# A weights' conversion on VectorE: shift and bitwise or in one instruction, for a shift and an integer addition

## The chip, the cores and the metric

The kernel runs on one core of one Trainium2 chip. The metric is device time in microseconds (us) for one execution of the whole program; where several executions are given, their median counts.

## The reference

Two parts follow each other. The first is a recurrent attention (RWKV-6): batch 4, 8 heads, 768 steps, 48 columns a head. The second is a dense block over the resulting 3072 tokens of 384 columns, with 2048 hidden columns. The weights of the dense block, `w_in` and `w_out`, arrive as 64-bit floats.

```python
for t in range(S):                       # for each batch b and head h
    y[t]  = r[t] @ (state + outer(u * k[t], v[t]))
    state = w[t][:, None] * state + outer(k[t], v[t])
x = y.transpose(...).reshape(3072, 384)
h = x @ w_in                             # 384 -> 2048
out = (h - tanh(h)) @ w_out              # 2048 -> 384
```

## The kernel before, in words

**Blocks.** The work is cut into 8 blocks of 384 tokens (4 batches, two halves of the sequence each). A block's dense part is a loop over `f` from 0 to 15, each `f` being 128 hidden columns. One step `f` does the following:

- TensorE multiplies the block's input by the weights `w_in` of this `f` (`first`, tile `hp`, L718: six matmuls of 128x384).
- ScalarE moves the product out of PSUM (tile `h`, L721). Only one `hp` tile exists, so the next step's `hp` matmuls need this move done.
- VectorE takes the square and its maximum (tile `s`, L747); ScalarE squares again (tile `qa`, L750); VectorE forms two products (tiles `h` and `sums`, both L724). The result approximates `h - tanh(h)`.
- Two steps later (`LAG`) TensorE multiplies this by `w_out` (`Second.add`, tile `acc`, L795: six matmuls).

In blocks 2 to 7 most of that second product uses fewer, recombined matmuls (L833). The change doesn't touch that.

**Attention between the steps.** While block `i` runs its dense loop, the attention of block `i+1` is spread over the same sixteen steps. The function `plan` says at which `f` each piece is issued: on VectorE the scans (L374, L385), products (L392, L399), the update of the states (L506, L516) and masked copies (L452); on ScalarE scalings (L410), copies (L471) and bounds (L416); on TensorE small matmuls (L445, L469, L494, L559, L576). A first stage, `boot`, does this for block 0 ahead of everything.

**The weights.** They are converted from 64-bit floats to 32-bit floats on the chip, once, slice by slice: `load_weights` (L240) brings slice `f`, 128 partitions x 768 numbers of 64 bits, as tile `raw` (five buffers), and `convert` turns it into `w_sb[:, f]`. ScalarE does three passes over 768 columns (all L253): the high word scaled into `w_sb`, the sign into the upper half of each word of tile `up`, and the low word, scaled and rounded to a small integer, into the lower half of `up`. VectorE then shifts `w_sb` left by 3 bits (L257) and adds `up` as integers (L258). Slices 0 to 2 are converted in `boot`, slice 3 begins there, and slices 4 to 15 are converted during block 0: at step `f` (from 1 on) ScalarE issues its three passes for slice `f + 3`, and VectorE's part is issued one step later, behind that step's square (L747). So `w_sb[:, 11]`, say, is finished on VectorE shortly before the `hp` matmuls of step 11 read it.

**Order.** The order of instructions on TensorE, VectorE, ScalarE and the SyncE queue is the order in which the program issues them (`manual_schedule`). Each engine works in order, and semaphores join the engines. The loads of later slices are held until the move `h` of their step (`begin_behind`).

Of the kernel before, what the change touches and what calls it, by code (L numbers as in the profile page):

```python
# [39 lines left out]
U32 = mybir.dt.uint32  # L40
# [5 lines left out]
AF = mybir.ActivationFunctionType  # L46
ALU = mybir.AluOpType
# [39 lines left out]
UPSCALE = 2.0 ** 8  # L87
HIGH_SCALE = 2.0 ** -111
SIGN_SCALE = 2.0 ** -64
LEAST = 2.0 ** -24  # L90


# [27 lines left out]
def kernel(  # L120
# [12 lines left out]
    nc = tc.nc  # L133
# [109 lines left out]
    def convert(f, raw, _):  # L243


        lo, hi = raw[:, :, 0], raw[:, :, 1]
        a = w_sb[:, f, :].bitcast(I32)
        up = conv.tile([P, 2 * DM], I32, name="up", tag="up", bufs=4)
        low, high = (up.bitcast(t).rearrange("p (n two) -> p n two", two=2)[:, :, i]
                     for i, t in enumerate((U16, F16)))  # L250

        def scaled(to, of, scale):
            return lambda: nc.scalar.activation(out=to, in_=of, func=AF.Copy, scale=scale)  # L253

        return [scaled(a.bitcast(F32), hi.bitcast(F32), HIGH_SCALE), scaled(high, hi.bitcast(F32), SIGN_SCALE),
                scaled(low, lo.bitcast(U32), 2.0 ** -29)], [
                lambda: nc.vector.tensor_single_scalar(a, a, 3, op=ALU.logical_shift_left),  # L257
                lambda: nc.vector.tensor_tensor(out=a, in0=a, in1=up, op=ALU.add)]  # L258

    def scratch(ps):  # L260
        return ps.tile([P, 2, BANK], F32, name="att", tag="att")
# [17 lines left out]
    class Block:  # L279
# [123 lines left out]
        def take_whole(self, p0, n):  # L403
            t = self.half("post", p0, n * NCH * LP).rearrange("d (c j) -> d c j", j=LP)[:, :, 1]
            nc.vector.tensor_single_scalar(self.whole(p0, n), t, LEAST, op=ALU.max)

# [12 lines left out]
        def held(self, p0, n):  # L419
            i = (self.b * NQ + self.q) * NPAIR * NCH  # L420
            nc.vector.tensor_single_scalar(holds[:, i + p0 * NCH:i + (p0 + n) * NCH], self.whole(p0, n), LEAST,
                                           op=ALU.is_gt)
# [506 lines left out]
    def boot(ps, blk, later):  # L929
# [34 lines left out]
        blk.times_before(h2, UP)  # L964
        blk.update_1(ps)
        first_a, first_b = convert(*raws.pop(0))
        second_a, second_b = convert(*raws.pop(0))
        third_a, third_b = convert(*raws.pop(0))
        run(first_a)
        own()  # L970
# [158 lines left out]
    for op in ahead_of_h + rest:  # L1129
        op()  # L1130
    nc.vector.tensor_single_scalar(again, sure[0:1, 0, 0:1], float(P * (n_whole + n_excess + n_top)),
                                   op=ALU.not_equal)
# [71 lines left out]
```

## Time and profile before

| what | value |
|---|---|
| time, median of 3 runs | 578.82 us (576.56 to 578.95) |
| time of the profiled execution | 575.73 us |
| its span, first to last instruction | 574.0 us |
| TensorE (PE) busy | 554.2 us, 97% |
| VectorE (DVE) busy | 486.3 us, 85% |
| ScalarE (ACT) busy | 345.4 us, 60% |
| granted TensorE clock | 1.000 |
| VectorE's shift, L257 | 16 times, 8.9 us |
| VectorE's integer addition, L258 | 16 times, 15.3 us |
| ScalarE's three passes, L253 | 48 times, 46.3 us |

The busy times belong to the whole span. All conversions lie between 16 and 92 us of it. A time in the profile is the duration of an instruction from its start to its end; two instructions on one engine can overlap a little, so that the distance from one start to the next is shorter than the duration.

### The profile page before, as it was taken

To read this page: it belongs to the slowest core of one execution; us is meant where nothing else is said; L and a number is where in the kernel's file an instruction comes from. 1 tells how busy PE (TensorE), PEld (TensorE's weight loads), DVE (VectorE), ACT (ScalarE), POOL (GpSimd) and SP (SyncE) were. 2 spreads that over 40 slices of the span, in tenths; PEclk is the share of its full clock that TensorE was granted. 3 is DMA by queue.
4 is the path that set the end of the run, shared out by engine and by line. 5 is a ranking of instruction groups with operands and counts; after the bars stand their busy time and mean duration, and the time that the engine had idled before them with its cause. 6 is when DMAs were issued, how large, how long until landed. Compare 5 with 4: busy or idle time off the path is not lost.

```text
span 574.0 us, 14058 instructions
## 1 busy us (share of the span) xinstructions
PE 554.2 (97%) x5736; PEld 405.6 (71%) x5736; DVE 486.3 (85%) x942; ACT 345.4 (60%) x702; POOL 11.9 (2%) x40
## 2 busy tenths in 40 slices
PE   4899999999999999999999999999999999999996
PEld 4646656566665787777878787778878777777763
DVE  8899995799979988979899898989999998658673
ACT  3889884433236765577565774767556775667441
POOL 6100000000000000000000000000000000000000
PEclk9999999999999999999999999999999999999999
DMA  8595454221302232032222232122221300100101
GB/s 312 184 377 175 166 166 123 82 83 56 112 12 84 83 112 61 8 120 62 58 65 83 84 106 63 53 82 70 88 66 49 120 2 2 44 10 1 42 2 45
DMA packets 32453, 50.40 MB, mean 88 GB/s; under 512 B 2560, under 2 KB 30336, under 8 KB 32384
## 3 DMA queue, kind: packets, MB, share of 16 engines
q1 hardware_dynamic: 32144, 49.38, 26.8%
q8 instruction: 46, 0.75, 0.5%
q14 instruction: 23, 0.19, 0.1%
q0 software_dynamic: 96, 0.07, 0.1%
q10 hardware_dynamic: 144, 0.00, 0.0%
HBM read 43.55 MB, written 4.72 MB: 84 GB/s over the span
## 4 chain that ended last, share of the span: by engine, by line
PE 87%; DVE 7%; ACT 3%; issue 1%; DMA 1%; SPq 0%; DVEq 0%
PE hp L718 40%; PE acc L833 22%; PE acc L795 10%; PE att L833 5%; PE att L445 3%; PE att L559 2%; PE att L494 2%; PE att L469 2%; PE att L576 2%; DVE w_sb L258 1%; ACT up L253 1%; DMA r<-in_rT 1%; DVE sums L724 1%; DVE w_sb L257 1%; DVE s L747 1%
## 5 line engine op out<-in xcount | busy, mean ns | idle before, releaser
L718 PE MATMUL hp<-xT,w_sb 128*128 128x384 f32 x768 | 270.3, 488 | 3.2 <-ACT h L721 1.4
L718 PEld LDWEIGHTS hp<-xT,w_sb 128*128 128x128 f32 x768 | 138.3, 190 | 83.6 <-ACT h L721 6.3
L721 ACT ACTIVATE h<-hp 128x384 f32<-128x384 f32 x128 | 62.6, 489 | 150.6 <-PE hp L718 149.2
L833 PE MATMUL acc<-forms,g 128*128 128x128 f32 x810 | 121.1, 277 | 0.5
L833 PEld LDWEIGHTS acc<-forms,g 128*128 128x128 f32 x810 | 108.7, 192 | 15.6 <-issue 1.2
L765 DVE TENSOR_TENSOR g<-g 128x256 f32<-128x256 f32 x225 | 95.5, 424 | 19.8 <-PE acc L833 0.9
L724 DVE SCALAR_TENSOR_TENSOR h<-h,s 128x384 f32<-128x384 f32 x128 | 70.4, 550 | 10.2 <-ACT s L739 9.6
L795 PE MATMUL acc<-w_sb,sums 128*128 128x384 f32 x192 | 68.0, 490 | 0.9 <-DVE sums L724 0.7
L724 DVE SCALAR_TENSOR_TENSOR g<-qa,h 128x384 f32<-128x384 f32 x96 | 53.6, 558 | 17.5 <-PE acc L833 4.0
L740 ACT ACTIVATE qa<-s,shift 128x384 f32<-128x384 f32 x90 | 55.4, 615 | 3.0
L742 ACT ACTIVATE junk<-s,shift 128x384 bf16<-128x384 f32 x90 | 53.9, 599 | 0.0
L795 PEld LDWEIGHTS acc<-w_sb,sums 128*128 128x128 f32 x192 | 35.7, 190 | 24.9 <-DVE sums L724 1.5
L739 ACT ACTIVATE s<-h 128x384 f32<-128x384 f32 x90 | 47.1, 523 | 2.8
L833 PE MATMUL acc<-w_sb,g 128*128 128x128 f32 x270 | 44.8, 275 | 0.0
L750 ACT ACTIVATE qa<-s,shift 128x384 f32<-128x384 f32 x38 | 23.4, 615 | 25.5 <-DVE top L747 25.5
L833 PEld LDWEIGHTS acc<-w_sb,g 128*128 128x128 f32 x270 | 37.4, 192 | 0.0
L253 ACT ACTIVATE up<-raw 128x768 f16<-128x768 f32 (+1 forms) x32 | 31.8, 1061 | 0.0
L747 DVE CUSTOM_DVE_ANT_0 s<-h 128x384 f32<-128x384 f32 x38 | 21.0, 553 | 11.6 <-ACT h L721 11.6
L833 PE MATMUL att<-w_sb,g 128*128 128x128 f32 x180 | 30.2, 275 | 0.0
L833 PEld LDWEIGHTS att<-w_sb,g 128*128 128x128 f32 x180 | 26.4, 192 | 4.5
L374 DVE TENSOR_TENSOR_SCAN pre<-w,start 128x780 f32<-128x780 f32 x16 | 28.5, 1782 | 0.6
L385 DVE TENSOR_TENSOR_SCAN post<-w,seed 128x780 f32<-128x780 f32 x16 | 28.5, 1783 | 0.1
(88 smaller groups left out, 529.3 us busy)
## 6 DMA issues: line engine op xcount, KB each, us to landing
raw<-in_weights SPq DMA_DIRECT2D x16, 768.0 KB, 4.5
w<-in_wT SPq DMA_DIRECT2D x7, 780.0 KB, 4.5
k<-in_kT SPq DMA_DIRECT2D x7, 768.0 KB, 4.6
r<-in_rT SPq DMA_DIRECT2D x7, 768.0 KB, 4.5
v_sb<-in_v SPq DMA_DIRECT2D x8, 576.0 KB, 4.3
k<-in_tokens SPq DMA_DIRECT2D x6, 576.0 KB, 3.9
r<-in_tokens SPq DMA_DIRECT2D x6, 576.0 KB, 3.9
out_y<-sums SPq DMA_DIRECT2D x15, 128.0 KB, 1.9
```

Source lines behind the costliest of these rows:

```text
L253: return lambda: nc.scalar.activation(out=to, in_=of, func=AF.Copy, scale=scale)
L374: return nc.vector.tensor_tensor_scan(out=self.tile("pre")[:, cols], data0=self.tile("w")[:, cols], data1=start[:, 0:n * NCH * LP], initia ...
L385: return nc.vector.tensor_tensor_scan(out=back(t[:, 0:width]), data0=back(self.tile("w")[:, a:a + width]), data1=back(seed[:, 0:width]), i ...
L718: nc.tensor.matmul(hp, lhsT=w_in_sb[:, f, kc, :], rhs=xT[kc], start=(kc == KC - 1), stop=(kc == 0))
L721: return h, nc.scalar.activation(out=h, in_=hp, func=AF.Copy, scale=1.0 / UPSCALE)
L724: return lambda: nc.vector.scalar_tensor_tensor(out=out, in0=in0, scalar=scalar, in1=in1, op0=op0, op1=ALU.mult)
L739: nc.scalar.activation(out=s, in_=h, func=AF.Square)
L740: nc.scalar.activation(out=qa, in_=s, func=AF.Square, bias=shift[:, 4:5])
L742: nc.scalar.activation(out=junk[:, 0:NB], in_=s, func=AF.Relu, bias=shift[:, 5:6], accum_out=excess[:, at:at + 1])
L765: return lambda: nc.vector.tensor_tensor(out=G[:, to:to + 2], in0=two(G, g_at(q, a0), g_at(q, a1)), in1=two(G, g_at(q, b0), g_at(q, b1)), ...
L795: nc.tensor.matmul(acc, lhsT=g[:, j * P:(j + 1) * P], rhs=w_out_sb[:, f, :], start=(f == self.first), stop=(f == NF - 1))
L833: nc.tensor.matmul(to, lhsT=G[:, g_at(q, a), :], rhs=rhs, start=start, stop=stop, skip_group_check=True)
```

## The change

The two VectorE instructions of `convert` become one, `scalar_tensor_tensor`, which shifts `w_sb` left by 3 and combines the result with `up` by a bitwise or. An addition lets the low word carry into the upper bits when it rounds up to 8; an or does not. So the low word is brought to 0 to 7: ScalarE's pass over it multiplies by 0.90625 x 2^-29 in place of 2^-29 and adds 0.2499, a constant inside the same instruction.

```diff
+LOW = 0.90625 * 2.0 ** -29, 0.2499
...
-        def scaled(to, of, scale):
-            return lambda: nc.scalar.activation(out=to, in_=of, func=AF.Copy, scale=scale)
+        def scaled(to, of, scale, bias=0.0):
+            return lambda: nc.scalar.activation(out=to, in_=of, func=AF.Copy, scale=scale, bias=bias)
 
         return [scaled(a.bitcast(F32), hi.bitcast(F32), HIGH_SCALE), scaled(high, hi.bitcast(F32), SIGN_SCALE),
-                scaled(low, lo.bitcast(U32), 2.0 ** -29)], [
-                lambda: nc.vector.tensor_single_scalar(a, a, 3, op=ALU.logical_shift_left),
-                lambda: nc.vector.tensor_tensor(out=a, in0=a, in1=up, op=ALU.add)]
+                scaled(low, lo.bitcast(U32), *LOW)], [
+                lambda: nc.vector.scalar_tensor_tensor(out=a, in0=a, scalar=3, in1=up, op0=ALU.logical_shift_left,
+                                                       op1=ALU.bitwise_or)]
```

VectorE's stream loses 16 instructions; the order of all others, and the streams of TensorE, ScalarE, GpSimd and SyncE, stay the same. From `convert` on, line numbers grow by two: L718 is L720 in the changed kernel.

## The prediction

> **What bounds the kernel now.** I read the busy times and slices first: which engine is full, and where.
>
> ```profile
> PE 554.2 (97%) x5736; PEld 405.6 (71%) x5736; DVE 486.3 (85%) x942; ACT 345.4 (60%) x702; POOL 11.9 (2%) x40
> ...
> PE   4899999999999999999999999999999999999996
> ...
> DVE  8899995799979988979899898989999998658673
> ```
>
> TensorE is full almost everywhere. The change acts only where conversions run, 24 to 92 us, so I next read stretches of 12 us there (busy us of each engine in brackets' order PE, weight load, DVE, ACT, POOL).
>
> ```profile
> 36.00:48.00 12.00, 11.30 (x43) 6.80 (x42) 11.62 (x20) 10.64 (x16) 0.00 (x0) 1.00 0.86 312
> 48.00:60.00 12.00, 11.95 (x112) 7.20 (x111) 11.49 (x21) 12.00 (x19) 0.00 (x0) 1.00 0.52 180
> 60.00:72.00 12.00, 11.73 (x127) 7.23 (x127) 11.21 (x25) 9.17 (x15) 0.00 (x0) 1.00 0.41 145
> 72.00:84.00 12.00, 10.66 (x124) 6.46 (x123) 11.41 (x23) 10.73 (x16) 0.13 (x2) 1.00 0.59 194
> ```
>
> Here VectorE runs without a pause, ScalarE is near full, and TensorE has gaps. The waits of 24 to 95 us say who ends them (columns: us in total, times, longest).
>
> ```profile
> ACT qa L750 <- DVE top L747: 4.7, 4, 2.6
> ...
> PE hp L718 <- DVE w_sb L258: 1.3, 1, 1.3
> ...
> PE acc L795 <- DVE sums L724: 0.7, 1, 0.7
> ```
>
> The two TensorE gaps end with VectorE: once the conversion itself is late, once a product queued behind a conversion. Where VectorE's time goes, the timeline shows (start us, duration us):
>
> ```profile
> 35.62 0.56 DVE L257 TENSOR_SCALAR w_sb<-w_sb 128x768 int32<-128x768 int32 x1
> 36.21 0.96 DVE L258 CUSTOM_DVE_ANT_0 w_sb<-w_sb,up 128x1536 uint16<-128x1536 uint16 x1
> 37.09 1.77 DVE L385 TENSOR_TENSOR_SCAN post<-w,seed 128x780 f32<-128x780 f32 x1
> ```
>
> From start to start, the shift holds VectorE for 36.21 - 35.62 = 0.59 us and the addition for 37.09 - 36.21 = 0.88: 1.47 a slice.
>
> **What the Trainium skill says.** (1) Vector Engine (DVE) Microarchitecture Reference, section 5.2 Measured stream behaviour on trn2: built-in one- and two-source ops take 1.0417 ns a column plus about 75 ns, on int32 streams. For 768 columns: 875 ns. The trace agrees for a two-source f32 op of 768 columns, `post` L399: 0.87 us from start to start (42.92 to 43.79). (2) The same page, section 7 Points that are easy to get wrong, has `S2S2D2_STT` (this form of instruction) halve its throughput with two non-bf16 sources. The trace doesn't agree for floats:
>
> ```profile
> L724 DVE SCALAR_TENSOR_TENSOR h<-h,s 128x384 f32<-128x384 f32 x128 | 70.4, 550 | 10.2 <-ACT s L739 9.6
> ...
> L399 DVE TENSOR_TENSOR post<-k,post 128x768 f32<-128x768 f32 x16 | 15.2, 947 | 0.0
> L257 DVE TENSOR_SCALAR w_sb<-w_sb 128x768 int32<-128x768 int32 x16 | 8.9, 555 | 0.0
> ```
>
> 550 ns for 384 columns and 947 for 768 lie on one line of 1.03 ns a column. No row shows it on integers. (3) ScalarE: Activation LUTs, section What ACT_TABLE_LOAD costs: immediate scale and bias cost nothing, a pointer operand about 93 ns. The trace fits: L740 with a bias operand takes 615 ns, L739 without one 523.
>
> **The change part by part.**
>
> - *Removed:* 16 shifts, 0.59 us each of VectorE's queue. *Replaced:* 16 additions at 0.88 by 16 combined passes. Low bound 0.88 (one column a tick; nothing suggests two[...]); high bound, by (2), 768 x 2 x 1.0417 + 75 = 1.68 us. I take 0.88, since the float form shows it. So VectorE gets 0.59 us a slice, 16 x 0.59 = 9.4 us in all, most of it beside TensorE's work.
> - *Low word's bias:* a constant in the instruction; the compiled ScalarE stream has the same instructions, without another operand. I take 0. If it did cost 93 ns, 16 x 0.093 = 1.5 us on ScalarE. Its waits for VectorE in this stretch are 4.7 us, so at most about half of that could reach TensorE, where ScalarE is full (48 to 60 us). A gain there has no mechanism.
> - *Waits:* VectorE's own wait between shift and addition goes (it is in the 0.59). The merged instruction needs all three ScalarE passes, where the shift needed the first. ScalarE ended the third before the conversion started by 1.70 us for slice 15 (88.39 against 90.09), 2.40 for slice 13, 2.24 for slice 3, 3 and more mostly. ScalarE moves forward too, as its 4.7 us of waiting are for VectorE. Nothing. Some `h` products gain a wait on VectorE's own `s`, one conversion (0.88 us) earlier: done by then. Nothing.
> - *Loads:* unmoved in SyncE's queue, but released by `h`, so they follow. The last slice's load is issued at about 77 us and takes 4.3 to land; ScalarE reads it at 85.61. Nothing, with some 4 us of cover. GpSimd's queue isn't passed.
>
> *What reaches TensorE.* I follow how far it runs ahead of its former times.
>
> 1. In `boot`, 24 to 31.6 us, VectorE waits for TensorE and ScalarE (0.62 us before 27.35), and its square at 31.64 can't start before `h` of step 0 is there at 31.51. Three conversions give 0.1.
> 2. The `acc` matmuls at 41.12 waited for `sums` (40.51), behind slice 3's conversion. `sums` comes 0.1 + 0.59 = 0.7 earlier. Lead **0.7**: all of the gap.
> 3. The `hp` at 52.49 started 0.2 late for ScalarE's `h`, in its full stretch. ScalarE had waited 1.10 and 0.26 for VectorE just before, and these go. Lead **0.9**. Here VectorE's gain is partly spent waiting for `qa` of ScalarE.
> 4. At 64.44, the `own` matmuls (L445) waited about 0.4 for the update of the states on VectorE to free their PSUM tile. VectorE is about 1.7 ahead by then. Lead **1.3**.
> 5. The `hp` of step 11:
>
> ```profile
> 73.94 2.10 PE L795 MATMUL acc<-w_sb,sums 128*128 128x384 f32 x6
> 77.38 2.17 PE L718 MATMUL hp<-xT,w_sb 128*128 128x384 f32 x6 [1.34 <-DVE w_sb L258]
> ```
>
> Six such matmuls start every 1.94 us when nothing holds them, so `hp` could start at 75.88; it lost 1.50 to slice 11's conversion, which ended at 77.24. With eight slices' 0.59, less what VectorE waits for ScalarE, VectorE is over 2 us ahead. Lead **2.8**.
>
> Later, TensorE waits for other engines only 1.2 us between 96 us and the end (two `hp` for `h`), so the lead is kept. What is late next is TensorE itself: from 36.38 to 94.34 it lost about 3.3 us in all (0.86 + 0.2 + 0.2 + 0.4 + 1.5 + 0.1), which is the most that can come back.
>
> Against the profiled execution: span 574.0 and 1.73 around it, 575.73; minus 2.8, 572.9. The median shown is 3.1 above this execution; 578.82 - 2.8 = **576.0 us**, 0.48% less.
>
> **The rivals.**
>
> - *ScalarE takes over.* With VectorE ahead, the chain `qa`, `h`, three passes sets the pace. For it: 12.00 of 12 us busy from 48 to 60, and its passes alone are 0.80 + 1.88 = 2.7 us of each step. Against: only 9.17 busy in the next stretch, and 2.59 of waiting there for VectorE. Step 2 stays and half of the rest comes: 0.7 + 1.0 = 1.7 or less, 577.1 to 578.1.
> - *The integer form is slow* (ends slower). At the half rate of (2) a slice costs 1.68, 0.21 above 1.47. Between 31 and 77 us ten conversions stand in VectorE's unbroken queue: 2.1 us later at step 11, and about 3 by the last slice, 581 to 582. It decides from 1.47 us a pass; it passes 0.5% above about 1.75. Against: the float form's 550 ns.
> - *It doesn't do what it says*, or it is hidden: the compiled stream has 16 instructions fewer, and the gaps end with VectorE, so a plain zero is unlikely.
> - *More than forecast:* all of the 3.3 us return, and `boot` gives a few tenths: 575.2.
>
> **How the numbers follow.** A measurement of this kernel can tell about 0.5%, 2.9 us, from no change; the forecast sits just at that edge. Forecast with its upper case: 0.70 (range alone 574.5 to 577.5, from 2.3 to 3.4 us and about 1 us of scatter between the runs shown). ScalarE takes over, or hidden: 0.15. Slow integer form, or a cost on VectorE not seen: 0.15. Of the first, I give 0.48 to faster by over 0.5% and 0.22 to within it; the second is all within, and of the third 0.03. So faster 0.48, same 0.40, slower 0.12. The range reaches from 3.4 us of gain with scatter, 573.9, to the rival of ScalarE with scatter, 579.3.
>
> **What the profile after would show.** Sixteen combined instructions of about 950 ns, 0.88 from start to start, and VectorE's busy time near 486.3 - 8.9 = 477.4. No gap of `hp` for `w_sb` at about 75, none before the second `acc`; ScalarE's wait for `top` in 24 to 95 us well under 4.7; TensorE's busy time unchanged and the span about 571.2. The low pass stays at 1054 ns. Wrong if the combined pass takes over 1.4 us, if TensorE's gaps stay with a new releaser (`h`, `qa`), or if a gap opens after 96 us.

## The result

The changed kernel takes 575.18 us (median of 12 runs, 572.83 to 577.45), the kernel before 577.68 (12 runs). The ratio, which is that of the means, is 0.9947, with a 95% interval of 0.9926 to 0.9968: 3.1 us faster, between 1.8 and 4.3 (the medians differ by 2.5). The same kernel run again on another occasion, beside the kernel before, gave 0.9958 (0.9943 to 0.9973).

The profiled execution of the changed kernel is a slow one for its kernel, 577.45 us and a span of 575.7, with TensorE's clock held down in the first 40 us, as it is in part of the executions of either kernel. So I don't compare spans, but the same stretch of work behind that start. **The stretch** runs from the start of step 1's `hp` to the start of step 14's `hp` of block 0 (steps count from 0; two expectations below call this last one step 15's). Its two ends, before and after:

```profile
31.56 2.20 PE L718 MATMUL hp<-xT,w_sb 128*128 128x384 f32 x6 [0.20 <-ACT h L721]
94.34 2.20 PE L718 MATMUL hp<-xT,w_sb 128*128 128x384 f32 x6
...
35.94 2.20 PE L720 MATMUL hp<-xT,w_sb 128*128 128x384 f32 x6 [0.20 <-ACT h L723]
96.18 2.20 PE L720 MATMUL hp<-xT,w_sb 128*128 128x384 f32 x6
```

That is 94.34 - 31.56 = 62.78 us before and 96.18 - 35.94 = 60.24 us after, 2.54 us less.

The page of the changed kernel: busy times, and the span in 40 equal slices, with the busy tenths of TensorE and VectorE and the tenths of full clock that TensorE was granted.

```profile
PE 554.9 (96%) x5736; PEld 405.4 (70%) x5736; DVE 477.6 (83%) x926; ACT 345.2 (60%) x702; POOL 11.9 (2%) x40
...
PE   4699999999999999999999999999999999999996
...
DVE  8669885699879998879999898999998998658673
...
PEclk9689999999999999999999999999999999999998
```

VectorE lost 8.7 us of busy time and 16 instructions; TensorE and ScalarE are busy within 0.7 us of before. The second and third slices of the clock, at 6 and 8 tenths, show the slow start. The stretches of 12 us, columns as before:

```profile
36.00:48.00 12.00, 11.37 (x35) 6.19 (x36) 11.18 (x19) 11.11 (x16) 0.00 (x0) 1.00 0.91 338
48.00:60.00 12.00, 12.00 (x122) 7.85 (x120) 10.78 (x19) 12.00 (x19) 0.00 (x0) 1.00 0.53 192
60.00:72.00 12.00, 12.00 (x129) 7.54 (x129) 10.04 (x26) 9.75 (x15) 0.00 (x0) 1.00 0.46 146
72.00:84.00 12.00, 12.00 (x129) 7.26 (x128) 11.03 (x20) 12.00 (x20) 0.13 (x2) 1.00 0.54 188
```

From 48 to 84 us TensorE has no gap; VectorE has some. Who waits (24 to 95 us):

```profile
DVE sums L726 <- ACT qa L752: 5.0, 6, 1.1
...
ACT qa L752 <- DVE top L749: 2.9, 2, 2.0
...
DVE sums L726 <- DVE h L726: 0.6, 1, 0.6
...
PE acc L797 <- DVE sums L726: 0.5, 1, 0.5
```

No `hp` matmul waits for VectorE's `w_sb` any more. ScalarE's wait for VectorE fell from 4.7 to 2.9 us, and VectorE now waits 5.0 us for ScalarE. One wait of TensorE for VectorE is left, before the second `acc`, and it hangs on a new wait of VectorE for itself. The timeline of VectorE there, first in the kernel before, then in the changed one, and a conversion in one pass with what follows it:

```profile
34.01 0.55 DVE L724 SCALAR_TENSOR_TENSOR h<-h,s 128x384 f32<-128x384 f32 x1
34.66 0.56 DVE L724 SCALAR_TENSOR_TENSOR sums<-qa,h 128x384 f32<-128x384 f32 x1
...
38.31 0.55 DVE L726 SCALAR_TENSOR_TENSOR h<-h,s 128x384 f32<-128x384 f32 x1
39.42 0.56 DVE L726 SCALAR_TENSOR_TENSOR sums<-qa,h 128x384 f32<-128x384 f32 x1 [0.56 <-DVE h L726]
...
45.62 0.95 DVE L259 SCALAR_TENSOR_TENSOR w_sb<-w_sb,up 128x768 int32<-128x768 int32 x1
46.49 0.95 DVE L401 TENSOR_TENSOR post<-k,post 128x768 f32<-128x768 f32 x1
```

The conversion holds VectorE for 46.49 - 45.62 = 0.87 us, where it held it for 1.47. The first `sums` starts 1.11 us after its `h` product; before, 34.66 - 34.01 = 0.65. And TensorE's own lines at the two places where it waited (the first line is of the kernel before, the others of the changed one):

```profile
41.12 2.20 PE L795 MATMUL acc<-w_sb,sums 128*128 128x384 f32 x6 [0.70 <-DVE sums L724]
...
45.28 2.20 PE L797 MATMUL acc<-w_sb,sums 128*128 128x384 f32 x6 [0.48 <-DVE sums L726]
...
77.28 2.10 PE L797 MATMUL acc<-w_sb,sums 128*128 128x384 f32 x6
79.22 2.18 PE L720 MATMUL hp<-xT,w_sb 128*128 128x384 f32 x6
```

Step 11's `hp` starts 1.94 us behind the piece ahead of it, without a wait. The second `acc` still waits.

### The profile page after: what moved, and what is told of

Same layout as the page of the kernel before. It is cut to its first block, busy times and chain, and to the rows that moved or that the text cites. A ratio compares the mean times of both kernels' runs of the same rounds, so it can differ in the third digit from the quotient of the medians.

```text
span 575.7 us, 14040 instructions
## 1 busy us (share of the span) xinstructions
PE 554.9 (96%) x5736; PEld 405.4 (70%) x5736; DVE 477.6 (83%) x926; ACT 345.2 (60%) x702; POOL 11.9 (2%) x40
## 4 chain that ended last, share of the span: by engine, by line
PE 93%; DVE 3%; issue 1%; DMA 1%; ACT 1%; SPq 0%; DVEq 0%; ACTq 0%
PE hp L720 42%; PE acc L835 21%; PE acc L797 13%; PE att L835 5%; PE att L447 3%; PE att L561 2%; PE att L578 2%; PE att L496 2%; PE att L471 2%; DMA r<-in_rT 1%; DVE post L387 1%; PE att L269 0%; DVE post L401 0%; DVE scores L454 0%; DVE pre L376 0%
## 5 line engine op out<-in xcount | busy, mean ns | idle before, releaser
L720 PE MATMUL hp<-xT,w_sb 128*128 128x384 f32 x768 | 270.4, 488 | 1.6 <-ACT h L723 1.4
L720 PEld LDWEIGHTS hp<-xT,w_sb 128*128 128x128 f32 x768 | 138.6, 191 | 81.9 <-ACT h L723 4.5
L726 DVE SCALAR_TENSOR_TENSOR sums<-qa,h 128x384 f32<-128x384 f32 x32 | 17.9, 558 | 15.6 <-ACT qa L752 12.2
## 6 DMA issues: line engine op xcount, KB each, us to landing
v_sb<-in_v SPq DMA_DIRECT2D x8, 576.0 KB, 4.3
k<-in_tokens SPq DMA_DIRECT2D x6, 576.0 KB, 3.9
r<-in_tokens SPq DMA_DIRECT2D x6, 576.0 KB, 4.0
```

Of the source, the lines that this page charges most:

```text
L720: nc.tensor.matmul(hp, lhsT=w_in_sb[:, f, kc, :], rhs=xT[kc], start=(kc == KC - 1), stop=(kc == 0))
L726: return lambda: nc.vector.scalar_tensor_tensor(out=out, in0=in0, scalar=scalar, in1=in1, op0=op0, op1=ALU.mult)
```

## The experiments

The theory: a slice takes 0.6 us less of VectorE's queue, and that closes gaps which TensorE had up to step 11. The rivals: the low word's pass or the new operation brings it; every slice counts alike; ScalarE or TensorE sets the pace anyway; the difference is the clock at the start. Ratios are to the kernel before, with 95% intervals; "stretch" is the one defined above, in one profiled execution each.

**The changed kernel again** (no edit).

> The changed kernel once more, beside the others on one chip. Theory (VectorE's queue: 0.59 us less a slice closes the gaps that TensorE had in block 0): ratio to the kernel before 0.993 to 0.997, and in a profile at full clock a span near 571.2 us, against 574.0. Rival (the difference seen was the granted clock of the first 40 us, which varies from run to run): ratio within 0.002 of 1 once runs of equal clock are compared.

Ratio 0.9958 (0.9943 to 0.9973), stretch 95.31 - 35.10 = 60.21 us. The profile at full clock that the expectation speaks of didn't come: this one had a clock of 0.993 and a span of 575.2. The stretch, in which the clock was 1.00 from 36 us on in both profiles, repeats to 0.03 us, so the gain in it is not the clock of the start. Executions of equal clock say the same of the whole: with a mean clock of 0.996 or 0.997 the changed kernel's spans here are 571.8 to 572.8 us (three) and those of the kernel before 574.2 to 576.4 (nine). The span near 571.2 us did appear in the first comparison, where the three executions of the changed kernel with a clock of 0.998 or more took 571.1 to 571.2; the ten of the kernel before with 0.999 or more took 573.9 to 574.4 on this occasion. The rival, the clock of the start, falls.

**Two passes, with an or.**

```diff
-                lambda: nc.vector.scalar_tensor_tensor(out=a, in0=a, scalar=3, in1=up, op0=ALU.logical_shift_left,
-                                                       op1=ALU.bitwise_or)]
+                lambda: nc.vector.tensor_single_scalar(a, a, 3, op=ALU.logical_shift_left),
+                lambda: nc.vector.tensor_tensor(out=a, in0=a, in1=up, op=ALU.bitwise_or)]
```

> Two passes on VectorE as before (shift, then a bitwise or of two tensors), with the low word brought to 0 to 7 as in the change. Theory (the number of passes counts): like before, ratio 0.998 to 1.002; about 1.47 us a slice on VectorE, the gap of hp ahead of step 11 back at 1.3 us. Rival (the low word's pass or the or in place of the custom addition brings the gain): ratio near 0.995. If the bias costs ScalarE anything, the ratio is above 1.002 and the low pass takes over 1.1 us.

Ratio 1.0013 (0.9998 to 1.0029), stretch 97.46 - 34.74 = 62.72 us: the kernel before, but for 0.06. The gap ahead of step 11 is back (first line). The low word's pass takes 1054 ns in the kernel before and 1059 in the changed one (the other lines), and 1055 here, where it has the bias too:

```profile
80.50 2.17 PE L720 MATMUL hp<-xT,w_sb 128*128 128x384 f32 x6 [1.36 <-DVE w_sb L260]
...
L253 ACT ACTIVATE up<-raw 128x768 uint16<-128x768 uint32 x16 | 16.9, 1054 | 0.0
...
L255 ACT ACTIVATE up<-raw 128x768 uint16<-128x768 uint32 x16 | 16.9, 1059 | 0.0
```

So neither the low word's bias nor the or in place of the integer addition does anything in this stretch; the number of passes does.

**One pass for slices 3 to 11 only, and for the others only.** The other slices take two passes (shift, then or).

```diff
-                scaled(low, lo.bitcast(U32), *LOW)], [
+                scaled(low, lo.bitcast(U32), *LOW)], ([
                 lambda: nc.vector.scalar_tensor_tensor(out=a, in0=a, scalar=3, in1=up, op0=ALU.logical_shift_left,
-                                                       op1=ALU.bitwise_or)]
+                                                       op1=ALU.bitwise_or)] if 3 <= f <= 11 else [
+                lambda: nc.vector.tensor_single_scalar(a, a, 3, op=ALU.logical_shift_left),
+                lambda: nc.vector.tensor_tensor(out=a, in0=a, in1=up, op=ALU.bitwise_or)])
```

The second kernel has `not 3 <= f <= 11` there.

> One pass for slices 3 to 11, two passes (shift, then or) for slices 0 to 2 and 12 to 15. Theory (what counts is VectorE's unbroken queue up to step 11): all of the gain, ratio 0.993 to 0.997 and within 0.001 of the changed kernel; TensorE's last gap may leave 0 to 0.3 us. Rival (every slice counts alike): nine sixteenths of the gain, ratio about 0.997.

> The complement: one pass for slices 0 to 2 and 12 to 15, two passes for 3 to 11. Theory: the gaps at the second acc, at the own matmuls and at step 11 stay, 0.1 us of gain, ratio 0.998 to 1.001. Rival (every slice counts alike): seven sixteenths of the gain, ratio about 0.998 and shorter gaps.

Slices 3 to 11: ratio 0.9949 (0.9929 to 0.9969), stretch 94.32 - 34.56 = 59.76 us, all of the gain and 0.48 us more than the change itself. The others: ratio 1.0024 (1.0010 to 1.0037), stretch 98.47 - 35.30 = 63.17 us, 0.39 *more* than before. So slices 3 to 11 carry the whole gain, which kills the rival in which every slice counts alike. But the complement missed its expectation (1.001 at most), and both stretches are off from the theory by some 0.4 us in the same sense: a cost goes with having slices 0 to 2 in one pass. A wait of VectorE shows it in the complement, as in the changed kernel:

```profile
38.78 0.56 DVE L728 SCALAR_TENSOR_TENSOR sums<-qa,h 128x384 f32<-128x384 f32 x1 [0.56 <-DVE h L728]
```

With slices 0 to 2 in two passes, that `sums` comes 37.58 - 36.92 = 0.66 us after its `h`. The complement's 0.24% is 1.4 us, of which 0.4 is in the stretch. In executions with a mean clock of 0.999 or more, its spans are 574.5 to 574.9 us (four) against 573.9 to 574.4 (ten) before, about those 0.4; the larger difference is in executions with a lower clock, and why it is larger there stays open.

**A third pass in the kernel before.**

```diff
                 lambda: nc.vector.tensor_single_scalar(a, a, 3, op=ALU.logical_shift_left),
+                lambda: nc.vector.tensor_single_scalar(a, a, 0, op=ALU.logical_shift_left),
```

> The kernel before with a third VectorE pass a slice (a shift by 0, 0.59 us), the suspected cost enlarged by the amount that the change takes away. Theory (VectorE's queue sets the pace of block 0): 13 slices from 3 to 15 make 7.7 us on VectorE, of which some 2.7 us of slack at the last slice's hp are covered: about 5 us slower, ratio 1.007 to 1.010. Rival (TensorE or ScalarE sets the pace, VectorE's passes lie beside them): under 1 us, ratio below 1.002.

Ratio 1.0094 (1.0078 to 1.0111), 5.4 us slower, as expected. The waits name the same two causes, now more often (third pass; us in total, times, longest), and the `own` matmuls wait too, for nothing that the profile names:

```profile
PE hp L719 <- DVE w_sb L259: 2.7, 4, 1.6
...
PE acc L796 <- DVE sums L725: 1.8, 2, 1.6
...
72.33 2.36 PE L446 MATMUL att<-r,k 48*64 48x64 f32 x96 [1.86 <-issue]
```

A shift more costs about twice what a shift less brings: VectorE's queue sets the pace at the gaps of the kernel before, and the next run shows what is left once they are closed. The size was reached by a wrong sum, though: before, slice 15 is ready at 91.64 us and step 15's `hp` starts at 98.31, a slack of 6.7 us and not 2.7. An estimate that fits is nine slices, 3 to 11, of 0.59 us, 5.3 us, all ahead of step 11's wait. (This profile's clock dipped to 0.86 of full in 72 to 84 us, so I take no stretch from it.)

**No pass on VectorE.** The conversion's list of VectorE operations is empty.

```diff
-                scaled(low, lo.bitcast(U32), *LOW)], [
-                lambda: nc.vector.scalar_tensor_tensor(...)]
+                scaled(low, lo.bitcast(U32), *LOW)], []
```

> VectorE's part of the conversion is left out altogether, so the weights stay unshifted and the output is of no use; all ScalarE passes are there. Theory (after the change TensorE and ScalarE bound block 0): only what TensorE still loses at the second acc and between parts comes back, 0.4 to 0.8 us beyond the changed kernel, ratio 0.992 to 0.995. Rival (VectorE still bounds): 0.88 us a slice more, 2 us and more beyond it, ratio below 0.991. Rival (ScalarE bounds): nothing beyond it, 0.995.

Ratio 0.9950 (0.9931 to 0.9969), stretch 93.86 - 34.46 = 59.40 us: 0.84 us under the changed kernel's 60.24, no 2 us. The total doesn't tell it apart from the changed kernel; the stretch does. From 48 to 60 us VectorE is busy 6.48 of 12 us, and from 24 to 100 us it waits 19.9 us for ScalarE's `qa`:

```profile
48.00:60.00 12.00, 12.00 (x116) 7.62 (x115) 6.48 (x14) 12.00 (x19) 0.00 (x0) 1.00 0.48 147
...
DVE sums L724 <- ACT qa L750: 19.9, 9, 5.5
```

So 59.40 is what TensorE and ScalarE leave; of the 3.4 us that VectorE's conversion cost in the stretch, the change took 2.54.

**A product moved behind the second `sums`.** In the changed kernel's `plan`:

```diff
-                      1: (..., "take_whole 0", "times_behind 2"),
-                      2: ("times_behind 0",), ...
+                      1: (..., "take_whole 0"),
+                      2: ("times_behind 2", "times_behind 0"), ...
```

> The changed kernel with one product of the attention (the times_behind of pairs 2 and 3, 0.87 us on VectorE) moved from step 1 to step 2, behind the second sums, which TensorE's second acc waits for. Theory: the last gap that VectorE causes, 0.48 us before the second acc, goes, and nothing new comes: 0.3 to 0.6 us faster than the changed kernel, ratio 0.992 to 0.995. Rival (ScalarE's chain in full stretch from 48 to 60 us takes it back): the gap moves to an hp behind h, ratio as the changed kernel's.

Ratio 0.9942 (0.9922 to 0.9962), stretch 96.12 - 36.08 = 60.04 us, 0.2 under the changed kernel. The second `acc` no longer waits, and step 6's `hp` does:

```profile
56.17 2.20 PE L720 MATMUL hp<-xT,w_sb 128*128 128x384 f32 x6 [0.25 <-ACT h L723]
```

About half of the 0.48 us is taken back by ScalarE, as the rival had it. The wait of the first `sums` stays (1.12 us after `h`).

**Memsets ahead, to move the first `sums` in VectorE's stream.** In the compiled stream the first `sums` stands three places earlier in all kernels so far with slices 0 to 2 in one pass, and there it waits; without any pass it stands six places earlier, and doesn't. So I put one or three tiny memsets at the start, into a tile that nothing reads; the third kernel joins the three memsets to the moved product.

```diff
     nc.vector.memset(ones, 1.0)
+    pad = const.tile([P, 3], F32, name="pad", tag="pad")
+    for i in range(3):
+        nc.vector.memset(pad[:, i:i + 1], 0.0)
```

> The changed kernel with one memset of a single column (59 ns) added at the start of VectorE's stream, where VectorE waits for its first load. It asks why the first sums comes 1.11 us after its h product in every kernel that converts slices 0 to 2 in one pass, and 0.66 in every other. Theory (it hangs on the place of that instruction in VectorE's stream, three places earlier with the change): a shift of one place may or may not move the wait, 0.66 or 1.11; where it moves, second acc starts 0.45 earlier after step 1's hp. Rival (it hangs on what goes ahead, the one-pass conversions or the wait for h): still 1.11.

> The same with three memsets, which bring the first sums back to its former place in VectorE's stream. Theory (place in the stream): 0.66 us from the h product to the first sums, the second acc's wait of 0.48 us gone, and 59.8 us from step 1's hp to step 15's hp, as in the kernel with one pass for slices 3 to 11 only (59.76), against 60.2 in the changed kernel. Rival (one-pass conversions of slices 0 to 2): 1.11 and 60.2 again.

> The three memsets together with the product moved behind the second sums. Theory (with the first sums in time, nothing that VectorE does holds TensorE): 59.4 to 59.8 us from step 1's hp to step 15's hp, the value without any VectorE pass being 59.4; ratio to the kernel before 0.992 to 0.996, 0.4 to 0.8 us below the changed kernel. Rival (ScalarE's chain, which held an hp for 0.25 us with the product moved, takes it back): 60.0.

With one memset or three, the wait is gone. VectorE with one:

```profile
35.74 0.55 DVE L729 SCALAR_TENSOR_TENSOR h<-h,s 128x384 f32<-128x384 f32 x1
36.41 0.56 DVE L729 SCALAR_TENSOR_TENSOR sums<-qa,h 128x384 f32<-128x384 f32 x1
```

0.67 us, and TensorE, with three:

```profile
40.14 2.10 PE L723 MATMUL hp<-xT,w_sb 128*128 128x384 f32 x6
42.26 2.20 PE L800 MATMUL acc<-w_sb,sums 128*128 128x384 f32 x6
```

The second `acc` follows 2.12 us behind step 3's `hp`, against 2.58 in the changed kernel. Stretches: 93.12 - 33.38 = 59.74 with one, 93.11 - 33.38 = 59.73 with three, 93.55 - 33.97 = 59.58 with the moved product as well. The one-pass conversions of slices 0 to 2 are all there, so they alone don't make the wait. The place in the stream fits all twelve profiles, but it isn't isolated: the memsets' tile also moves later tiles in memory, and the kernel with one pass for slices 3 to 11, where nothing moved in memory and the wait is missing too, has other conversions ahead. What lies behind the wait isn't shown. Nor is it shown that it is there at full clock, where no kernel that has it was profiled: with a mean clock of 1.000 the changed kernel has a span of 571.1 us and the kernel with slices 3 to 11 in one pass 571.0, one execution each on two occasions, which leaves little room for the 0.48 us between their stretches.

The first two ran once each (574.88 and 574.39 us), so they have no ratio. The third was timed: 0.9945 (0.9922 to 0.9967). In the stretch it is 0.66 us better than the change; in the whole time the two can't be told apart, and I don't claim that it beats the changed kernel.

## Why the prediction was right, and where it was off

The total: 2.8 us or 0.48% was forecast, 3.1 us (1.8 to 4.3) and, the second time, 2.4 us (1.6 to 3.3) were measured. The forecast time of 576.0 us counted from a median of three runs, 578.82, that was 1.1 above the median of twelve; from 577.68, the same 2.8 us give 574.9, against 575.18 measured. By its steps:

- **The pass.** 0.88 us from start to start was taken, of a bracket of 0.88 to 1.68; it is 0.87, and 953 ns long. The rival of a slow integer form falls, and with it, for this instruction, the halving that the Trainium skill's Vector Engine (DVE) Microarchitecture Reference states in section 7, Points that are easy to get wrong. The estimate of 875 ns from its section 5.2, Measured stream behaviour on trn2 (1.0417 ns a column and about 75 ns), fits the 0.87 us. The shift alone doesn't follow it: over the same 768 columns it took 0.59 us, so the saving is that shorter pass and not a half of the conversion. VectorE's busy time: 477.4 forecast, 477.6 measured.
- **The low word's bias.** Nothing was taken. The low pass takes 1059 ns for 1054, with two passes 1055, and the kernel with the bias and two passes has the stretch of before to 0.06 us.
- **The lead, step by step.** Counted from the start of step 1's `hp`, TensorE is ahead of the kernel before by:

| place | forecast | changed kernel | with three memsets |
|---|---|---|---|
| second `acc` | 0.7 | 9.56 - 9.34 = 0.22 | 9.56 - 8.88 = 0.68 |
| step 6's `hp` | 0.9 | 20.93 - 20.44 = 0.49 | 0.96 |
| `own` matmuls | 1.3 | 32.88 - 31.94 = 0.94 | 1.40 |
| step 11's `hp` | 2.8 | 45.82 - 43.28 = 2.54 | 3.01 |
| step 14's `hp`, end of the stretch | 2.8 | 2.54 | 3.05 |

The step that failed is the second of the prediction's list: "`sums` comes 0.1 + 0.59 = 0.7 earlier. Lead **0.7**: all of the gap." It came 0.2 earlier, since the first `sums`, ahead of it in VectorE's queue, waited 0.45 us longer than before. All later steps carry that deficit along, and with the memsets the forecast's leads stand to 0.25 us. The third, fourth and fifth of the list each gained a little more than forecast, 0.27, 0.45 and 1.60 us for 0.2, 0.4 and 1.5. So the list is right in kind, but that the stretch comes within 0.3 us of the forecast is in part luck: these three gave back 0.22 of the 0.48 that the second lacked.

- **What remains.** The bound of 3.3 us for all that TensorE lost fits the kernel without any VectorE pass, which is 62.78 - 59.40 = 3.38 ahead.
- **The rival of ScalarE** is half there. It holds VectorE (5.0 us of waits for `qa`) and takes back part of what the moved product gained, but TensorE, with no gap from 48 to 84 us, doesn't feel it in the changed kernel.
- **Waits and loads taken at nothing** stayed so: no wait of a conversion for `up` or of ScalarE for `raw` appears from 24 to 95 us, and between 96 us and the end TensorE's waits are 1.2 us, as before. The tenth of a us from `boot` can't be seen beside the start's scatter.
- **A count.** For the slow integer form I put ten conversions between 31 and 77 us; the trace of before has nine (35.62 to 75.68), so that rival would have cost 1.9 us at step 11 and not 2.1.
- **Chances.** The forecast put itself at the edge of 0.5%; the two ratios fall on both sides of it.

## What to carry to other kernels

Where an engine is full on average but not in one stage, follow its lead over the other engines from wait to wait in that stage: 9.4 us of VectorE's queue became 2.5 us of TensorE's, all of it from the nine slices ahead of the last wait. Put experiments on the stage (a fixed stretch between two instructions of the bounding engine) where the total scatters by more than the effect: two profiles of the changed kernel agreed to 0.03 us in the stretch, while its totals ranged over 3.4 and 4.6 us within twelve runs. And a merged instruction can move others in their stream: look in the new trace for a wait that no dependence explains.

## What the runs showed that I had not expected

- A wait of 0.45 us on VectorE between two dependent instructions, in all four profiles in which the second one stood three places earlier in the stream, and in none of the other eight, with the dependence itself unchanged. In the changed kernel, `qa`, its other input, was ready at 38.23 us, 1.19 us ahead of it. Its cause is open.
- TensorE's clock at the start differs from profile to profile: from 24 to 36 us it was 0.61 and 0.72 of full in two profiles of the changed kernel, 1.00 in the one of the kernel before, and 0.59 at the least. Step 1's `hp` started between 31.56 us (clock 1.00) and 36.08 us (0.59), a spread that is larger than the change is worth. The 44 executions of the kernel before that ran beside the changed kernel on the second occasion show it in the whole: spans of 573.9 to 574.4 us at a mean clock of 1.000, and of 575.6 to 578.3 us at 0.989.
